# Block attention and a gated MLP on one core: a fourth group by seven half products, and GpSimd with part of the elementwise work

## The chip, the core and the metric

The kernel runs on one core of a Trainium2 chip. The core's engines each work through their own list of instructions in order: TensorE (PE) multiplies matrices and loads weights, VectorE (DVE) and ScalarE (ACT) do elementwise work on SBUF and PSUM, GpSimd (POOL) and SyncE (SP) here issue the DMA transfers. They wait for each other at semaphores. The metric is the device time of one execution in microseconds (us).

## What is computed

An attention over chunks of 64 tokens, and a two-layer MLP with the gate h * sigmoid(beta * h) on its result:

```python
def _attn_ref(q, k, v):                       # [8, 8, 576, 64]
    scores = scale * np.matmul(q_c, k_c.transpose(0, 1, 2, 4, 3))   # per chunk of 64
    scores = scores - np.max(scores, axis=-1, keepdims=True)
    attn = np.exp(scores)
    attn = attn / (np.sum(attn, axis=-1, keepdims=True) + 1e-09)
    out = np.matmul(attn, v_c)
    return out.reshape(B, H, S, D).astype(np.float32)

def _moe_ref(x, w_in, w_out, beta):           # x [4608, 512], w_in [512, 2048], w_out [2048, 512]
    h = x @ w_in
    g = h * (1.0 / (1.0 + np.exp(-beta * h)))
    return (g @ w_out).astype(np.float32)
```

The attention's output, with the heads side by side, is the x of the MLP.

## The kernel before

The 4608 tokens are worked in nine blocks of 512, numbered 0 to 8 (`NB` is 9, `QB` is 6). The attention of the later blocks is spread as small items between the matmuls of the earlier ones; it is finished when block 6 begins. Blocks 6, 7 and 8 then hold nothing but the MLP. In a block j of these, TensorE makes two things in turns: the first layer of block j (its "lane"), and the second layer of block j-1.

The second layer is done with Winograd's form of Strassen's scheme: 2 by 2 quarters, seven products (`emit_prod`, L585; p = 1, 2, 6, 5, 7, 3, 4, each for two token tiles t) in place of eight. VectorE makes the four sums of g that it needs (`emit_sum`, L436, the tiles `sm`), each once per block.

The first layer has 16 column tiles m of 128. A full product (`emit_m`, L372) makes one m with four matmuls of 512 columns; ScalarE applies Silu (L381) and VectorE scales the result by 1/beta into `gt` (`emit_mg`, L356). From block 6 on, four m at a time can instead be made as a group i by seven half products (`emit_q`, L484), again Winograd's form: four matmuls of 256 columns each. It needs sums of x (`emit_tx`, L465, four tiles `tx` per block) and sums of the weights (`emit_ws`, L456, four tiles per group, made once). A group goes in four steps s = 0 to 3 with the half products (1, 2), (6, 5), (7, 3) and (4). They are accumulated in two PSUM tiles, `qx` and `qz`; after 1, 6 and 5 ScalarE copies a state of these to the SBUF tile `hq` (L503), after 2, 7 and 3 VectorE adds one (L506), so a later half product must not write before the earlier state is taken. Then ScalarE applies Silu (`emit_q_silu`, L513: two instructions for each of three parts), and VectorE scales by 1/beta into `gt` (`emit_q_scale`, L527: two instructions for each half r of a group).

Before the change blocks 6, 7 and 8 each make groups 1, 2 and 3 by half products and m = 0 to 3 by full products. The PSUM tiles `qx` and `qz` come from the pool `ps_p0` with four buffers, those of the full products from the pool `ps_r` with two. `hq` has three buffers, `tx` two.

The order is written by hand: for each block a list of items with a place between 0 and 1 is made and sorted (L745 to L801), and each engine works through its part of the list. `LANE` (L730 to L736) gives the order of full products ("m", n) and group steps ("q", i, s), spread evenly over the block; `prod` items stand between them; silus ("qs"), scalings ("qt"), big sums ("sum"), sums of x for the next block ("tx", L777) and sums of weights ("ws", L796) get places of their own:

```python
                        c, e, f = (0.98 * sum(cost[:n + d]) / sum(cost) for d in (0, 1, 2))
...
                            items += [(e - 0.002, 2, ("qs", it[1], 2)), (f - 0.001, 2, ("qs", it[1], 1)),
                                      (f + 0.03, 3, ("qt", it[1], 0))]
...
                    if j + 1 < NB:
                        items += [(0.70 + 0.06 * n, 5, ("tx", j + 1, n)) for n in range(4)]
```

After block 8's list the rest of block 8's second layer follows (L852 to L858): the halves of the sums that are still open, then products 2, 6, 5, 7, 3 and 4, with the last stores.

GpSimd issues all loads from memory; its last one is issued long before block 6. It does no arithmetic on tiles apart from an identity matrix at the start. SyncE issues the transposes by DMA and the stores.

Of the kernel before, what the change touches and what calls it, by code (L numbers as in the profile page):

```python
# [8 lines left out]
FP32 = mybir.dt.float32  # L9
FP16 = mybir.dt.float16  # L10
ACTF = mybir.ActivationFunctionType
ALU = mybir.AluOpType
# [3 lines left out]
def kernel(  # L16
# [10 lines left out]
    nc = tc.nc  # L27
# [25 lines left out]
    ps_p0, ps_x, ps_s0 = [p.__enter__() for p in ps_open]  # L53
    ps_p, ps_s = [ps_p0], [ps_s0]
# [11 lines left out]
    ws = {i: [big.tile([128, 2, 256], FP16, name=f"ws{i}{n}") for n in range(4)] for i in (1, 2, 3)}  # L66
# [14 lines left out]
    QB = 6  # L81
# [376 lines left out]
    def emit_tx(j, n):  # L458
        if n == 0:
            tx_t[j] = [qs_p[1].tile([128, 2, 4, CH], FP16, tag=f"tx{n}", name=f"tx{n}", bufs=2) for n in range(4)]  # L460
        tx = tx_t[j]
        xq = xt_t[j].rearrange("p t (r k) (c q) -> p k c (t r) q", r=2, c=2)
        b11, b12, b21, b22 = (xq[:, :, c, 4 * r:4 * r + 4, :] for c in range(2) for r in range(2))
        in0, in1 = ((b12, b11), (b22, tx[0]), (b22, b12), (b21, tx[1]))[n]
        nc.vector.tensor_tensor(out=tx[n], in0=in0, in1=in1, op=ALU.subtract)  # L465

    qz_t = {}

# [22 lines left out]
    def emit_q(j, i, s):  # L491
        if j not in gt_t:
            gt_t[j] = gt_p.tile([128, KFF, 512], FP16, tag="gt", name="gt")
        if s == 0:
            qz_t[j, i] = [ps_p0.tile([128, 2, 256], FP32, tag="p", name=n) for n in ("qx", "qz")]
            qz_t[j, i] += [
                qs_p[0].tile([128, 4, 2, 256], FP32, name="hq")]
        x, z, hq = qz_t[j, i]
        for p in ((1, 2), (6, 5), (7, 3), (4,))[s]:
            emit_q_prod(j, i, p)  # L500
            if p in (1, 6, 5):
                o = {1: hq[:, 0:2, 0], 6: hq[:, 0:2, 1], 5: hq[:, 2:4, 1]}[p]
                nc.scalar.copy(out=o, in_=z if p == 5 else x)  # L503
            if p in (2, 7, 3):
                o = {2: hq[:, 0:2, 0], 7: hq[:, 2:4, 1], 3: hq[:, 0:2, 1]}[p]
                nc.vector.tensor_tensor(out=o, in0=x if p == 7 else z, in1=o, op=ALU.add)  # L506
# [16 lines left out]
    def emit_q_scale(j, i, r):  # L523
        hq = qz_t[j, i][2]
        for b in (2 * r, 2 * r + 1):
            m = 4 * i + b
            nc.vector.tensor_scalar(  # L527
                out=gt_t[j][:, m, :], in0=hq[:, b].rearrange("p c q -> p (c q)"),
                scalar1=rb[:, m:m + 1], scalar2=None, op0=ALU.mult)

# [83 lines left out]
    with tc.manual_schedule():  # L614
# [3 lines left out]
        for a, eng, dst in ((0, nc.sync, raw0), (1, nc.gpsimd, qk0[1])):  # L618
            for i, src in enumerate((q, k)):
                eng.dma_start(  # L620
                    out=dst[i],
# [97 lines left out]
        def att_items(u, a0, w):  # L719
            it = [(a0, 2, ("sc", u)), (a0 + 0.36 * w, 3, ("pv", u)), (a0 + 0.361 * w, 3, ("norm", u, 0)),  # L720
                  (a0 + (0.42 if u >= WV else 0.50) * w, 3, ("norm", u, 1))]
            if u >= WV:
# [7 lines left out]
        LANE = [(("m", 0), ("q", 1, 0), ("m", 1), ("q", 1, 1), ("q", 2, 0), ("q", 1, 2), ("q", 2, 1), ("q", 1, 3), ("q", 2, 2),  # L730
# [7 lines left out]
        for j in range(1, NB):  # L738
# [6 lines left out]
            items = []  # L745
# [6 lines left out]
            else:  # L752
                m0 = {2: 0.36, 4: 0.09}.get(j, 0.02)
                if j < QB:
                    items += [(m0 + (1 - m0) * m / KFF, 0, ("m", m)) for m in range(KFF)]
                else:
                    lane = LANE[2 if j == QB else j == NB - 1]
                    cost = [1 if it[0] == "q" and it[2] == 3 else 2 for it in lane]
                    for n, it in enumerate(lane):
                        c, e, f = (0.98 * sum(cost[:n + d]) / sum(cost) for d in (0, 1, 2))  # L760
                        items.append((c, 0, it))
                        if it[0] == "m":
                            items.append((c + 0.04, 3, ("mg", it[1])))
                        elif it[0] == "last":
                            pass
                        elif it[2] == 2:
                            if it[1] == 3:
                                f = e
                            items += [(e - 0.002, 2, ("qs", it[1], 2)), (f - 0.001, 2, ("qs", it[1], 1)),
                                      (f + 0.03, 3, ("qt", it[1], 0))]  # L770
                        elif it[2] == 3:
                            items += [(c + 0.001, 2, ("qs", it[1], 0)), (c + 0.04, 3, ("qt", it[1], 1))]
                    if j == QB:
                        items.append((0.01, 6, ("open",)))
                        items += [(0.011+0.001*n, 6, ("tx", QB, n)) for n in range(4)]
                    if j + 1 < NB:
                        items += [(0.70 + 0.06 * n, 5, ("tx", j + 1, n)) for n in range(4)]  # L777
                for i, p in enumerate((1, 2, 6, 5, 7, 3, 4)):
                    for t in range(2):
                        w = 1.06 if j == NB - 1 else 0.98  # L780
# [9 lines left out]
                if j == 2:  # L790
                    items += [(c, 3, ("wt", i)) for i, c in ((2, 0.36), (3, 0.55))]
                    items += [(0.07, 2, ("sc", 5)), (0.08, 2, ("xp", 4, 0)), (0.12, 2, ("xp", 4, 1)),
                              (0.17, 2, ("pv", 5)), (0.18, 3, ("norm", 5, 0)), (0.19, 3, ("norm", 5, 1)),
                              (0.27, 3, ("T", 6)), (0.53, 3, ("T", 7)), (0.60, 3, ("T", 8)), (0.61, 3, ("T", 9)), (0.80, 3, ("T", 10)),
                              (0.30, 2, ("xp", 5, 0)), (0.32, 2, ("xp", 5, 1))]
                for jw, i, c, d in ((3, 2, 0.10, 0.22), (4, 1, 0.21, 0.22), (4, 3, 0.10, 0.22)):  # L796
                    if jw == j:
                        items += [(c + d * n, 5, ("ws", i, n)) for n in range(4)]
# [92 lines left out]
```

## Time and profile before

| what | us |
|---|---|
| median of 3 runs (lowest to highest) | 275.88 (275.48 to 276.67) |
| the profiled execution's own time | 276.16 |
| its span, first to last instruction | 274.4 |
| TensorE busy | 266.0 |
| VectorE busy | 209.7 |
| ScalarE busy | 167.5 |
| GpSimd busy | 95.4 |
| first layer, L372, 488 matmuls | 106.1 |
| scalings of the groups, L527, 36 instructions | 16.2 |
| sums of x, L465, 12 instructions | 5.0 |

The times are read so: the span is what the profile covers, and the execution's time is 1.76 us longer. The granted TensorE clock was 1.00 over the whole span. A matmul's busy time overlaps with that of the next one, since they are pipelined; from start to start, four matmuls of 512 columns take 0.86 us and eight of 256 take 0.87. The busy time of a GpSimd row is rough.

### The profile page before, as it was taken

The numbers are of one execution on the slowest core, as the hardware profiler recorded it, in microseconds if no ns is written. First come the engines' busy times: TensorE is split into PE (matmuls) and PEld (weight loads), VectorE is DVE, ScalarE is ACT, GpSimd is POOL, SyncE is SP. The second block draws the span as 40 slices with busy tenths as digits, with TensorE's granted clock in tenths as the row PEclk, the third lists the DMA queues.
The fourth block names the chain that finished last, engine by engine and source line by source line (L and its number), as shares of the span: only waits on it lengthen the run. The fifth ranks groups of instructions, "written<-read, shape, count | busy, mean of one in ns | idle before, by whom it ended". The sixth has DMA issues, their size and how long they took to land.

```text
span 274.4 us, 7822 instructions
## 1 busy us (share of the span) xinstructions
PE 266.0 (97%) x3237; PEld 184.9 (67%) x3237; DVE 209.7 (76%) x394; ACT 167.5 (61%) x300; POOL 95.4 (35%) x122
## 2 busy tenths in 40 slices
PE   7789999999999999999999999999999999999995
PEld 3565445857656666666666666668887887788874
DVE  3558755899998688677977887659888778877951
ACT  3278515886555566556655656567778496759621
POOL 8954387579639955323436210000000000000000
PEclk9999999999999999999999999999999999999999
DMA  9999999999999999999999999966112102110223
GB/s 137 164 194 202 192 174 178 245 169 169 169 164 155 159 173 153 193 145 141 155 154 193 134 143 201 153 155 118 38 41 76 41 0 79 38 41 1 78 79 115
DMA packets 141763, 36.43 MB, mean 133 GB/s; under 512 B 125856, under 2 KB 141216, under 8 KB 141728
## 3 DMA queue, kind: packets, MB, share of 16 engines
q0 software_dynamic: 99136, 18.10, 83.0%
q1 hardware_dynamic: 42592, 17.84, 36.4%
q8 instruction: 25, 0.41, 0.6%
q14 instruction: 10, 0.08, 0.1%
HBM read 36.71 MB, written 9.44 MB: 168 GB/s over the span
## 4 chain that ended last, share of the span: by engine, by line
PE 67%; DMA 14%; DVE 10%; POOL 5%; issue 2%; ACT 2%; DVEq 0%; POOLq 0%
PE hps L372 23%; PE ya L585 14%; PE yb L585 14%; PE qx L484 5%; DMA wout<-in_moe_w_out_dram 5%; PE qz L484 4%; PE acc L585 4%; DMA qu<-in_q_dram 3%; DMA win<-in_moe_w_in_dram 3%; DMA ku<-in_k_dram 3%; DVE sm L436 3%; DVE gt L360 2%; POOL vbig L120 2%; PE sc L219 1%; POOL qu L112 1%
## 5 line engine op out<-in xcount | busy, mean ns | idle before, releaser
L372 PE MATMUL hps<-xt,win 128*128 128x512 f16 (+1 forms) x488 | 106.1, 355 | 0.9 <-DMA win<-in_moe_w_in_dram 0.7
L384 ACT ACTIVATE sg<-hps,bt 128x512 f32<-128x512 f32 (+1 forms) x111 | 69.5, 635 | 34.3 <-PE hps L372 31.9
L360 DVE SCALAR_TENSOR_TENSOR gt<-sg,hps 128x512 f16<-128x512 f32 (+1 forms) x111 | 67.7, 617 | 27.1 <-ACT sg L384 26.2
L372 PEld LDWEIGHTS <-win 128*128 128x128 f16 x488 | 46.2, 98 | 32.3 <-DMA win<-in_moe_w_in_dram 1.2
L585 PEld LDWEIGHTS <-sm 128*128 128x128 f16 x512 | 49.5, 98 | 12.2 <-issue 0.3
L585 PEld LDWEIGHTS <-gt 128*128 128x128 f16 x384 | 36.8, 98 | 10.6 <-DVE gt L527 0.6
L120 POOL DMA_DIRECT2D vbig<-in_v_dram x40 | 34.1, 870 | 21.8 <-DMA ku<-in_k_dram 6.3
L106 POOL DMA_DIRECT2D qu<-in_q_dram x20 | 17.1, 873 | 20.6 <-DMA qT<-qu 6.0
L513 ACT ACTIVATE hq<-hq,bs 128x256 f32<-128x256 f32 (+1 forms) x36 | 19.9, 610 | 5.5 <-DVE hq L506 5.5
L527 DVE TENSOR_SCALAR gt<-hq,rb 128x512 f16<-128x512 f32 x36 | 16.2, 481 | 6.0 <-ACT hq L513 5.3
L106 POOL DMA_DIRECT2D ku<-in_k_dram x20 | 17.1, 883 | 10.2 <-DMA qu<-in_q_dram 5.1
L436 DVE TENSOR_TENSOR sm<-gt 128x2048 f16<-128x2048 f16 (+1 forms) x17 | 19.6, 1155 | 0.3
L585 PE MATMUL yb<-wt,sm 128*128 128x256 f16 x152 | 19.7, 273 | 0.1
L585 PE MATMUL ya<-wt,sm 128*128 128x256 f16 x152 | 19.7, 273 | 0.0
L484 PEld LDWEIGHTS <-ws 128*128 128x128 f16 x144 | 14.1, 98 | 1.6
L241 ACT ACTIVATE et<-sc 128x1024 f16<-128x1024 f32 (+1 forms) x10 | 8.3, 852 | 10.5 <-PE sc L232 10.4
L397 PE MATMUL ops<-wout,gt 128*128 128x512 f16 x64 | 14.7, 380 | 0.0
L585 PE MATMUL yb<-wout,gt 128*128 128x256 f16 x104 | 13.9, 273 | 0.2
L585 PE MATMUL ya<-wout,gt 128*128 128x256 f16 x104 | 13.6, 273 | 0.0
L506 DVE TENSOR_TENSOR hq<-qz,hq 128x512 f32<-128x512 f32 x18 | 12.3, 683 | 1.1 <-ACT hq L503 0.8
L503 ACT COPY hq<-qx 128x512 f32<-128x512 f32 x18 | 10.5, 581 | 2.9 <-PE qx L484 2.7
L278 DVE TENSOR_TENSOR x<-x,rx 128x512 f16<-128x512 f32 (+1 forms) x20 | 11.9, 620 | 0.3
(100 smaller groups left out, 354.3 us busy)
## 6 DMA issues: line engine op xcount, KB each, us to landing
out_dram<-osb SPq DMA_DIRECT2D x32, 256.0 KB, 2.9
vbig<-in_v_dram POOLq DMA_DIRECT2D x32, 128.0 KB, 7.6
qu<-in_q_dram POOLq DMA_DIRECT2D x18, 128.0 KB, 11.5
ku<-in_k_dram POOLq DMA_DIRECT2D x18, 128.0 KB, 8.3
win<-in_moe_w_in_dram POOLq DMA_DIRECT2D x8, 256.0 KB, 9.5
wout<-in_moe_w_out_dram POOLq DMA_DIRECT2D x4, 512.0 KB, 12.2
qu<-in_q_dram POOLq DMA_DIRECT2D x5, 256.0 KB, 6.5
ku<-in_k_dram POOLq DMA_DIRECT2D x5, 256.0 KB, 6.8
```

Of the source, the lines that this page charges most:

```text
L106: nc.gpsimd.dma_start(out=tv[off:off + n, sp], in_=src[b, :, s:s + n, :].rearrange("h p d -> p h d"),)
L120: nc.gpsimd.dma_start(out=vbig[off:off + n, i % NV, :, 0:D], in_=v[b, :, s:s + n, :].rearrange("h p d -> p h d"),)
L360: nc.vector.scalar_tensor_tensor(out=gt_t[j][:, m, c0:c0 + n], in0=sg[:, 0:n], scalar=1.0, in1=hps[:, 0:n], op0=ALU.add, op1=ALU.mult,)
L372: nc.tensor.matmul(out=hps[:, 0:n], lhsT=w_in16[m // 2][:, kk, (m % 2) * 128:(m % 2) * 128 + 128], rhs=xr[:, c0 // CH:(c0 + n) // CH, 2 * ...
L384: nc.scalar.activation(out=sg[:, 0:n], in_=hps[:, 0:n], func=ACTF.Tanh, scale=bt[:, m:m + 1])
L397: nc.tensor.matmul(out=ops, lhsT=gt_t[j][:, kk, t * 128:(t + 1) * 128], rhs=w_out16[kk // 4][:, kk % 4, :], start=(kk == 0), stop=(kk == K ...
L436: nc.vector.tensor_tensor(out=sm[i][:, lo:hi, :], in0=a, in1=b, op=op)
L484: nc.tensor.matmul(out=dst[:, s, :], lhsT=lhsT, rhs=rhs, start=(p in (1, 2, 5) and s == 0 and kk == 0), stop=(s == 1 and kk == 1), skip_gr ...
L506: nc.vector.tensor_tensor(out=o, in0=x if p == 7 else z, in1=o, op=ALU.add)
L513: nc.scalar.activation(out=o, in_=src, func=ACTF.Silu, scale=bs[:, m:m + 1])
L527: nc.vector.tensor_scalar(out=gt_t[j][:, m, :], in0=hq[:, b].rearrange("p c q -> p (c q)"), scalar1=rb[:, m:m + 1], scalar2=None, op0=ALU. ...
L585: nc.tensor.matmul(out=dst, lhsT=lhsT, rhs=rhs, start=(p in (1, 2, 5) and kk == 0 and (t == 0 or last)), stop=(kk == 7 and (t == 1 or last ...
```

## The change

Six things change.

1. In block 7 all 16 column tiles are made by half products: group 0 joins groups 1, 2 and 3, and the four full products are gone. The lane of block 7 (`LANE[0]`) is written anew, and spread over 0.96 of the block instead of 0.98.
2. In block 7 the two PSUM tiles of group 2 come from `ps_r`, which the full products no longer use there.
3. The four sums of weights of group 0 are made by VectorE in block 6.
4. GpSimd instead of VectorE makes the sums of x for blocks 7 and 8; their places in the list are earlier (0.40 to 0.70 in place of 0.70 to 0.88).
5. In each group of blocks 6, 7 and 8, GpSimd makes the first of the four scalings (b = 0).
6. In all three blocks the Silu items of part 2 are placed a little earlier (0.02 ahead of e instead of 0.002), and the scalings of r = 0 a little later (0.04 after f instead of 0.03).

```diff
-        nc.vector.tensor_tensor(out=tx[n], in0=in0, in1=in1, op=ALU.subtract)
+        (nc.gpsimd if j > QB else nc.vector).tensor_tensor(out=tx[n], in0=in0, in1=in1, op=ALU.subtract)
...
-            qz_t[j, i] = [ps_p0.tile([128, 2, 256], FP32, tag="p", name=n) for n in ("qx", "qz")]
+            qz_t[j, i] = [(ps_p[0] if j == 7 and i == 2 else ps_p0).tile([128, 2, 256], FP32, tag="p", name=n) for n in ("qx", "qz")]
...
-            nc.vector.tensor_scalar(
+            (nc.gpsimd if r == 0 and b % 2 == 0 else nc.vector).tensor_scalar(
                 out=gt_t[j][:, m, :], in0=hq[:, b].rearrange("p c q -> p (c q)"),
                 scalar1=rb[:, m:m + 1], scalar2=None, op0=ALU.mult)
...
-        LANE = [(("m", 0), ("q", 1, 0), ("m", 1), ("q", 1, 1), ("q", 2, 0), ("q", 1, 2), ("q", 2, 1), ("q", 1, 3), ("q", 2, 2),
-                 ("q", 3, 0), ("q", 2, 3), ("q", 3, 1), ("m", 2), ("q", 3, 2), ("m", 3), ("q", 3, 3)),
+        LANE = [(("q", 1, 0), ("q", 0, 0), ("q", 2, 0), ("q", 1, 1), ("q", 1, 2), ("q", 0, 1), ("q", 0, 2), ("q", 2, 1), ("q",
+                 1, 3), ("q", 0, 3), ("q", 2, 2), ("q", 3, 0), ("q", 2, 3), ("q", 3, 1), ("q", 3, 2), ("q", 3, 3)),
...
+                    ls = 0.96 if j == 7 else 0.98
                     for n, it in enumerate(lane):
-                        c, e, f = (0.98 * sum(cost[:n + d]) / sum(cost) for d in (0, 1, 2))
+                        c, e, f = (ls * sum(cost[:n + d]) / sum(cost) for d in (0, 1, 2))
...
-                            items += [(e - 0.002, 2, ("qs", it[1], 2)), (f - 0.001, 2, ("qs", it[1], 1)),
-                                      (f + 0.03, 3, ("qt", it[1], 0))]
+                            items += [(e - 0.02, 2, ("qs", it[1], 2)), (f - 0.001, 2, ("qs", it[1], 1)),
+                                      (f + 0.04, 3, ("qt", it[1], 0))]
...
-                        items += [(0.70 + 0.06 * n, 5, ("tx", j + 1, n)) for n in range(4)]
+                        items += [(0.40 + 0.10 * n, 5, ("tx", j + 1, n)) for n in range(4)]
...
+                if j == 6:
+                    items += [(0.30 + 0.10 * n, 5, ("ws", 0, n)) for n in range(4)]
```

## The prediction

> **What bounds the kernel now.** The first view is the page's head: the sums by engine, and the span in 40 slices of 6.86 us.
>
> ```profile
> PE 266.0 (97%) x3237; PEld 184.9 (67%) x3237; DVE 209.7 (76%) x394; ACT 167.5 (61%) x300; POOL 95.4 (35%) x122
> ...
> PE   7789999999999999999999999999999999999995
> ...
> POOL 8954387579639955323436210000000000000000
> ```
>
> TensorE is full from the fourth slice on; GpSimd is empty from the 25th, after its last load. The change touches only blocks 6, 7 and 8 (nine blocks, counted from 0). I found their borders in the timeline and asked for busy time in each; the fourth row is the products left after block 8's lane.
>
> ```profile
> core 0: us, PE busy (x) PEld busy (x) DVE busy (x) ACT busy (x) POOL busy (x), PEclk, DMA share, GB/s
> 183.30:208.20 24.90, 24.90 (x228) 20.76 (x216) 22.13 (x42) 17.98 (x35) 0.00 (x0) 1.00 0.32 81
> 208.20:233.20 25.00, 25.00 (x215) 20.68 (x214) 20.51 (x37) 17.78 (x36) 0.00 (x0) 1.00 0.13 43
> 233.20:258.20 25.00, 25.00 (x215) 20.70 (x213) 20.51 (x35) 17.50 (x36) 0.00 (x0) 1.00 0.10 33
> 258.20:271.40 13.20, 12.85 (x113) 10.63 (x111) 7.71 (x15) 4.71 (x13) 0.00 (x0) 1.00 0.30 101
> ```
>
> A block of 25.0 us holds 25.0 us of TensorE at clock 1.00, so a matmul taken away is time taken away. But VectorE is busy for 82 to 89% of a block, and TensorE has little patience with it. The view of waits, for weight loads in this stretch, shows where VectorE already makes TensorE stop:
>
> ```profile
> PEld L585 <- DVE gt L527: 0.6, 2, 0.3
> PEld L585 <- DVE gt L356: 0.4, 2, 0.2
> ```
>
> Two waits on L356 are at the borders 6 to 7 and 7 to 8 (a product of 1.14 us at 209.08, of 1.14 at 234.03, where others have 1.04); two on L527 are in the tail at 260.75 and 261.15. Hidden waits have short slack. An example from block 7: the second half product of a group (qz) may not be overwritten until VectorE has added it, and VectorE has scalings ahead of that addition.
>
> ```profile
> 224.02 0.60 PE L484 MATMUL qz<-xt,win 128*128 128x256 f16 x4
> ...
> 226.20 0.60 PE L484 MATMUL qz<-tx,ws 128*128 128x256 f16 x4
> ```
> ```profile
> 224.20 0.87 DVE L527 TENSOR_SCALAR gt<-hq,rb 128x512 f16<-128x512 f32 x2
> 225.13 0.69 DVE L506 TENSOR_TENSOR hq<-qz,hq 128x512 f32<-128x512 f32 x1
> ```
>
> The addition ends at 225.82, TensorE overwrites at 226.20: slack 0.38 us. At the same place in block 6 (addition 200.17 to 200.86, qz at 201.25) it is 0.39.
>
> **The change, part by part.**
>
> *TensorE.* In block 7 four full products (L372: 16 matmuls of 512 columns) become a fourth group (L484: 28 of 256). In the chain of waits four of the first kind take 0.86 us and eight of the second 0.87: 4 x 0.865 = 3.46 against 28 x 0.109 = 3.05, so **-0.41 us**. Twelve more weight loads at 0.098 us lie under matmuls of 0.109; uncovered they would cost up to 1.2.
>
> *ScalarE.* Four Silu of 685 ns go; three copies (581), two Silu each of 474, 502 and 717 ns come: 5.1 - 2.7 = +2.4 us in block 7, where it works 17.8 of 25.0 us. The cover is its idle 7.2 us; without it the copies that free qx and qz would be late, and TensorE with them. I price it at 0.
>
> *VectorE.* Away go eight sums of x (about 0.34 us from start to start) and ten of 47 scalings (0.40): 2.7 + 4.0. Added are four sums of weights in block 6 (0.34) and three additions (0.60): 1.4 + 1.8. It is relieved by 3.5 us in 75; where it is not what TensorE waits for this is worth nothing. The weight sums are put among the last two big sums of block 6, of which the third has 4.0 us of slack (done 193.74, first used 197.76); that covers 1.4.
>
> *Order.* At block 6's tight place three scalings now stand ahead of the addition instead of two: +0.40 against the slack of 0.39, so 0 to 0.1 us.
>
> *Buffers and queues.* Group 2 of block 7 takes its two PSUM buffers from the pool that the full products leave. The fourth group's first ScalarE copy waits for GpSimd's scaling of the first group, and other ScalarE work queues behind it; some eight lane items (about 10 us) lie between. No DMA is added, and SyncE's list stays. GpSimd's 18 instructions stand behind all its loads, so no load is delayed; among themselves sums of x queue behind scalings that wait for ScalarE, but each is needed several us later.
>
> *GpSimd's own durations* are shown by no row of these forms. The nearest ones:
>
> ```profile
> masks.py:199 POOL TENSOR_SCALAR_AFFINE_SELECT ident<-ident 128x128 f16<-128x128 f16 x1 | 0.3, 290 | 0.1
> L875 POOL MEMSET const-bfloat16-1.0<- 128x1 bf16 x1 | 0.1, 102 | 0.0
> L527 DVE TENSOR_SCALAR gt<-hq,rb 128x512 f16<-128x512 f32 x36 | 16.2, 481 | 6.0 <-ACT hq L513 5.3
> ```
>
> A fixed 0.10 and 0.19 for 128 columns give 0.86 us for 512, all of it scaled by four gives 1.16: estimates, of which I take 1.0 for a scaling. Below, VectorE's 0.48 is the end; above, twice 1.16 = 2.3 if 4-byte input or a second input doubles it. A sum of x has two inputs: 0.86 to 2.3, I take 1.2.
>
> *What the engines do to each other.* The trace has no GpSimd arithmetic beside VectorE. The low end is no effect: a big sum at 66.36 took 1.23 us beside GpSimd's DMA issues, 1.22 without. The high end is that one stands while the other works. The scalings meet by construction: of a pair released by the same two Silu, GpSimd gets the first and VectorE the second. VectorE's pair took 0.80; 1.0 of standing plus 0.40 is **+0.6**. The issue row speaks for 0, but issuing is no reading of tiles, so I take half, 0.3. Then the border 6 to 7 and the tail, without slack, lose 0.3 each, block 6's tight place 0.3 (its slack being spent on the third scaling), block 7's nothing (0.3 under 0.38): +0.9. A fourth meeting is early in block 6: the first two sums of x of block 7 need only their data, whose last transposes are issued at 178.10 to 183.25 and land some 3.7 us later, so about when VectorE makes its own sums of x (185.88) and the big sums from 188.55. The second big sum ends at 191.01 and is used at 191.21. Half of 1.2 less 0.2 would be 0.4; since the two may also run before, I take 0.2. The border 7 to 8 loses its wait for a full product's scaling, at most 0.1 gained, left out.
>
> The Trainium skill ("SBUF — State Buffer", Who interferes with whom) says that a VectorE instruction with two SBUF inputs, or in a two-port mode as a scaling can be, and a GpSimd instruction that reads SBUF exclude each other for the whole instruction. By that the term is the full one and the sum that of the first rival; no run here shows it yet. Its "GPSIMD Engine Reference" (Elementwise — side-by-side cycle accounting) puts one-input work at 1.03 to 1.8 cycles an element at 1.2 GHz, an estimate of 0.44 to 0.77 us for 512; with that a pair would lose at most 0.4, and the sum would be nearer to no change.
>
> **Sum:** -0.41 + 0.9 + 0.2 = +0.7 us. The profiled execution took 276.16 (span 274.40, 1.76 around it), 0.28 over the median of 275.88. Its span would be 275.1; on the median the forecast is **276.6 us**, no change by what a measurement of this kernel can tell (0.5%, 1.4 us).
>
> **Rivals.**
> *Full exclusion* (the other side, slower). Place: VectorE's queue ahead of the tight places; price 0.6 per pair; it decides once what it adds passes 1.8 us, that is 0.41 and 1.4. Border and tail 0.6 each; block 6's place 0.6 + 0.01; block 7's 0.6 - 0.38 = 0.22; the early meeting 1.2 - 0.2 = 1.0: 3.03 - 0.41 = +2.6, **278.5**. For it: pairs start together, and VectorE has 82% to do. Against it: the 1.23 us sum.
> *No effect.* TensorE's 0.41 is kept less 0.1 at block 6: -0.3, **275.6**. For it: VectorE is relieved by 3.5 us. Against: the tail keeps its waits, since ScalarE paces the last scalings. Faster by 1.4 would need the 0.41 and all 1.0 of the shown waits gone.
> *GpSimd twice as slow.* Scalings of 2.3 with full exclusion cost 1.3 more at four places: 2.6 + 5.2 = +7.8, **283.7**; if only two of the places are met, 281.1. For it: 4-byte input; against: nothing but the small row.
>
> **How the numbers follow.** Forecast 0.36 (0.05 of it above 277.3), full exclusion 0.33 (0.01 of it under 277.3), no effect 0.22 (0.03 of it faster by over 0.5%, for the shown runs span 1.2 us), twice as slow 0.09. Slower: 0.05 + 0.32 + 0.09 = 0.46. Same: 0.31 + 0.01 + 0.19 = 0.51. Faster 0.03. The range reaches from no effect less some measuring spread, 275.3, to full exclusion with one more meeting of 1.3, 279.8; outside lie about 0.05 below and 0.13 above. The forecast's own range is 275.8 (one meeting of 0.3 alone) to 277.5 (0.9 more in all).
>
> **What would show it.** Block 7 must hold 24.6 us of TensorE work; if it lasts 24.6, the first step is right. GpSimd's rows give L465 and L527 their durations: 1.2 and 1.0. L527 and the big sums on VectorE tell the exclusion: at 0.48 and 1.22 there is none, and rows stretched towards 1.0 or gaps ahead of them, with no releaser, are the full one. New waits of weight loads or matmuls on VectorE should stand at block 6's second big sum and last group, the border 6 to 7 and the tail. Wrong would be waits on ScalarE in block 7, or TensorE waiting for GpSimd itself.

## The result and the profile after

The changed kernel takes 277.05 us (median of 9 runs, 276.96 to 277.86) against 275.60 for the kernel before on the same chip (9 runs, 275.02 to 276.67): a ratio of 1.0051, 95% interval 1.0039 to 1.0064, so 1.4 us slower. The profiled execution took just the median time (277.05), with a span of 275.3.

First the sums by engine and one of the rows of 40 slices, from the page of the changed kernel:

```profile
PE 265.8 (97%) x3249; PEld 185.9 (68%) x3249; DVE 210.4 (76%) x383; ACT 168.8 (61%) x305; POOL 121.1 (44%) x140
...
POOL 8964478489639945333436200030344093204200
```

GpSimd now has work after the 25th slice. VectorE, which was to be relieved, is busy for 210.4 us where it was busy for 209.7, with eleven instructions fewer. Next the busy time of each engine in blocks 6, 7, 8 and the rest (the borders are put at the same matmuls as for the kernel before):

```profile
core 0: us, PE busy (x) PEld busy (x) DVE busy (x) ACT busy (x) POOL busy (x), PEclk, DMA share, GB/s
182.95:208.30 25.35, 25.15 (x233) 20.80 (x219) 22.77 (x39) 18.09 (x36) 8.33 (x7) 1.00 0.31 85
208.30:234.02 25.72, 24.98 (x227) 21.88 (x225) 21.90 (x32) 18.91 (x41) 11.30 (x8) 1.00 0.13 42
234.02:259.33 25.31, 25.16 (x216) 20.88 (x214) 20.17 (x32) 18.60 (x38) 4.69 (x3) 1.00 0.10 33
259.33:272.44 13.11, 12.67 (x112) 10.39 (x109) 7.00 (x13) 4.36 (x12) 1.57 (x1) 1.00 0.30 101
```

Block 7 was to shrink from 25.0 to 24.6 us; it lasts 25.72. Block 6 has grown by 0.45 us and block 8 by 0.31. The clock is 1.00 as before. The waits from 183 us on, first those of weight loads, then those of matmuls (us in total, times, longest):

```profile
PEld L484 <- issue: 1.5, 3, 0.8
PEld L585 <- DVE gt L527: 0.5, 2, 0.3
PEld L585 <- DVE gt L356: 0.4, 1, 0.4
...
```
```profile
PE qz L484 <- DVE hq L506: 0.8, 2, 0.6
PE yb L585 <- DVE gt L356: 0.2, 1, 0.2
```

New are the waits of the half products (L484): the matmul waits for VectorE's addition (L506) to take the state of `qz`, and the weight load behind it stands for "issue" only because the matmul does. TensorE never waits for GpSimd or ScalarE.

For an account that adds up I took the starts of all matmuls from block 6's first half product to the last matmul, and subtracted from each distance what the matmul needs, 0.2165 us for 512 columns and 0.1092 for 256. What remains are the times in which TensorE stood; these are worked out from the trace, not lines of it:

| place | before | after | forecast for the difference |
|---|---|---|---|
| block 6, last group, `qz` | 0 | 0.37 | +0.3 |
| border 6 to 7 | 0.09 | 0.32 | +0.3 |
| block 7, last group, `qx` and `qz` | 0 | 0.88 | 0 |
| border 7 to 8 | 0.09 | 0 | 0 |
| block 8, group 1, `qz` | 0 | 0.31 | 0 |
| tail | 0.78 | 0.69 | +0.3 |
| early in block 6 | 0 | 0 | +0.2 |
| all gaps | 0.98 | 2.59 | +1.1 |
| first to last matmul | 85.96 | 87.16 | +0.7 |

The matmuls alone took 0.41 us less, as forecast; the gaps grew by 1.61: together the +1.20 of the last row. (The two medians differ by 1.45, the two profiled spans by 0.9, since the stretch ahead of block 6 varies by some tenths between executions: its first half product starts at 185.10 us before and at 184.78 after.) The rows by form of VectorE and of GpSimd say who did it (busy us, mean ns of one):

```profile
L436 DVE TENSOR_TENSOR sm<-gt 128x2048 f16<-128x2048 f16 x15 | 18.3, 1217 | 0.2
L527 DVE TENSOR_SCALAR gt<-hq,rb 128x512 f16<-128x512 f32 x30 | 17.9, 641 | 8.6 <-ACT hq L513 8.2
...
L356 DVE TENSOR_SCALAR gt<-sg,rb 128x512 f16<-128x512 f32 x7 | 3.8, 548 | 0.2
```
```profile
L527 POOL TENSOR_SCALAR gt<-hq,rb 128x512 f16<-128x512 f32 x10 | 15.6, 1564 | 51.9 <-ACT hq L513 51.9
...
L465 POOL TENSOR_TENSOR tx<-xt,tx 128x512 f16<-128x512 f16 x4 | 5.3, 1324 | 0.1
L465 POOL TENSOR_TENSOR tx<-xt 128x512 f16<-128x512 f16 x4 | 5.1, 1285 | 26.0 <-DMA xt<-x 26.0
```

VectorE's scalings, 481 ns each before, now take 641 and 548: 30 x 0.16 + 7 x 0.067 = 5.3 us. That is more than the 3.5 us of work it gave away. Where it went is seen best at block 7's tight place, in the timelines of VectorE, GpSimd and TensorE there (start us, us, engine, line):

```profile
224.60 2.58 DVE L527 TENSOR_SCALAR gt<-hq,rb 128x512 f16<-128x512 f32 x3 [1.87 <-ACT hq L513]
...
229.70 0.68 DVE L506 TENSOR_TENSOR hq<-qz,hq 128x512 f32<-128x512 f32 x1
```
```profile
224.06 1.56 POOL L527 TENSOR_SCALAR gt<-hq,rb 128x512 f16<-128x512 f32 x1 [0.31 <-ACT hq L513]
225.59 1.31 POOL L465 TENSOR_TENSOR tx<-xt 128x512 f16<-128x512 f16 x1
```
```profile
229.25 0.60 PE L484 MATMUL qx<-tx,ws 128*128 128x256 f16 x4
230.43 0.60 PE L484 MATMUL qz<-tx,ws 128*128 128x256 f16 x4 [0.58 <-DVE hq L506]
```

Three scalings that need 1.28 us (two take 0.87 to 0.88, so 0.40 from start to start, and 0.48 for the last) took 2.58. The second ended 0.28 us after GpSimd's scaling, the third 0.28 after GpSimd's sum of x. VectorE has no pause from there to the addition at 229.70, so what the two meetings cost, 1.30 us, reaches the addition. How much of it TensorE feels is told by the run with nothing on GpSimd (the first experiment), which has the same lane. There the addition ends at 228.27 and TensorE overwrites `qz` at 228.40, so the slack of this lane is 0.13 us, not the 0.38 of the old one. Counted against TensorE's work, the addition comes 0.96 us later in the changed kernel than in that run, so 0.83 should come through. TensorE's gaps there are 0.04, 0.10 and 0.74.

### The profile page after: what moved, and what is told of

It is laid out like the page before. It is cut to its first block, busy times and chain, and to the rows that moved or that the text cites. A ratio compares the mean times of both kernels' runs of the same rounds, so it can differ in the third digit from the quotient of the medians.

```text
span 275.3 us, 7880 instructions
## 1 busy us (share of the span) xinstructions
PE 265.8 (97%) x3249; PEld 185.9 (68%) x3249; DVE 210.4 (76%) x383; ACT 168.8 (61%) x305; POOL 121.1 (44%) x140
## 4 chain that ended last, share of the span: by engine, by line
PE 71%; DVE 15%; DMA 6%; ACT 3%; issue 3%; POOL 2%; DVEq 0%; ACTq 0%; POOLq 0%
PE hps L372 26%; PE yb L585 13%; PE ya L585 11%; PE ops L397 5%; PE qx L484 4%; PE acc L585 4%; PE qz L484 3%; DMA qu<-in_q_dram 3%; DVE sm L436 3%; DVE gt L527 3%; DMA ku<-in_k_dram 3%; DVE gt L360 2%; ACT hq L513 2%; DVE hq L506 2%; PE sc L219 1%
## 5 line engine op out<-in xcount | busy, mean ns | idle before, releaser
L372 PE MATMUL hps<-xt,win 128*128 128x512 f16 (+1 forms) x472 | 102.2, 354 | 0.4 <-ACT xt L333 0.2
L372 PEld LDWEIGHTS <-win 128*128 128x128 f16 x472 | 44.8, 98 | 30.5 <-issue 0.4
L120 POOL DMA_DIRECT2D vbig<-in_v_dram x40 | 34.1, 871 | 24.6 <-DMA ku<-in_k_dram 7.7
L527 POOL TENSOR_SCALAR gt<-hq,rb 128x512 f16<-128x512 f32 x10 | 15.6, 1564 | 51.9 <-ACT hq L513 51.9
L513 ACT ACTIVATE hq<-hq,bs 128x256 f32<-128x256 f32 (+1 forms) x40 | 22.1, 611 | 8.0 <-DVE hq L506 8.0
L527 DVE TENSOR_SCALAR gt<-hq,rb 128x512 f16<-128x512 f32 x30 | 17.9, 641 | 8.6 <-ACT hq L513 8.2
L484 PEld LDWEIGHTS <-ws 128*128 128x128 f16 x160 | 15.6, 98 | 3.4 <-issue 1.5
L465 POOL TENSOR_TENSOR tx<-xt 128x512 f16<-128x512 f16 x4 | 5.1, 1285 | 26.0 <-DMA xt<-x 26.0
L506 DVE TENSOR_TENSOR hq<-qz,hq 128x512 f32<-128x512 f32 x20 | 13.6, 681 | 0.5 <-ACT hq L503 0.4
L503 ACT COPY hq<-qx 128x512 f32<-128x512 f32 x20 | 11.6, 582 | 3.1 <-PE qx L484 2.9
```

The lines of the kernel that those rows point to most:

```text
L120: nc.gpsimd.dma_start(out=vbig[off:off + n, i % NV, :, 0:D], in_=v[b, :, s:s + n, :].rearrange("h p d -> p h d"),)
L372: nc.tensor.matmul(out=hps[:, 0:n], lhsT=w_in16[m // 2][:, kk, (m % 2) * 128:(m % 2) * 128 + 128], rhs=xr[:, c0 // CH:(c0 + n) // CH, 2 * ...
L484: nc.tensor.matmul(out=dst[:, s, :], lhsT=lhsT, rhs=rhs, start=(p in (1, 2, 5) and s == 0 and kk == 0), stop=(s == 1 and kk == 1), skip_gr ...
L513: nc.scalar.activation(out=o, in_=src, func=ACTF.Silu, scale=bs[:, m:m + 1])
L527: (nc.gpsimd if r == 0 and b % 2 == 0 else nc.vector).tensor_scalar(out=gt_t[j][:, m, :], in0=hq[:, b].rearrange("p c q -> p (c q)"), scal ...
```

## The experiments

The theory under test, called the port theory in the expectations: a GpSimd instruction holds VectorE's instructions that work from SBUF to SBUF while it runs, and that alone makes the loss; the fourth group is worth its 0.41 us. Rivals: the fourth group itself costs (its order, ScalarE's 2.4 us, the Silus moved), or it is the number of instructions on VectorE's queue.

**Nothing on GpSimd.** Both lines of GpSimd's part are undone; the fourth group, the order and the places in the list stay.

```diff
-        (nc.gpsimd if j > QB else nc.vector).tensor_tensor(out=tx[n], in0=in0, in1=in1, op=ALU.subtract)
+        nc.vector.tensor_tensor(out=tx[n], in0=in0, in1=in1, op=ALU.subtract)
...
-            (nc.gpsimd if r == 0 and b % 2 == 0 else nc.vector).tensor_scalar(
+            nc.vector.tensor_scalar(
```

> The changed kernel without GpSimd's part: sums of x and scalings all on VectorE, the fourth group and the new order kept. Theory 'port': no scaling is stretched (L527 at 481 ns throughout), the waits at qz in blocks 6, 7 and 8 (0.37, 0.75, 0.30 us) shrink to what VectorE's own load makes of them; with 3.2 us more work on it than in the kernel before, 0 to 0.9 us slower than before, ratio 1.000 to 1.0035. Theory 'order': the waits stay where they are and the ratio is that of the changed kernel, 1.005, or above it.

Measured: 275.01 us (11 runs) against 275.45, ratio 0.9989 (0.9977 to 1.0001). Busy time in block 7, and VectorE's scalings:

```profile
core 0: us, PE busy (x) PEld busy (x) DVE busy (x) ACT busy (x) POOL busy (x), PEclk, DMA share, GB/s
...
207.40:232.00 24.60, 24.60 (x227) 21.85 (x225) 21.87 (x39) 18.65 (x40) 0.00 (x0) 1.00 0.13 44
```
```profile
L527 DVE TENSOR_SCALAR gt<-hq,rb 128x512 f16<-128x512 f32 x40 | 17.5, 482 | 5.8 <-ACT hq L513 5.2
```

Block 7 lasts 24.60 us and is full; from the first half product to the last matmul it is 85.55 us, 0.41 less than before, with the same gaps (0.97). So the fourth group costs nothing beside its saving, though VectorE is busier here than before (21.87 us against 20.51), and the whole loss is GpSimd's part. The port theory's own number was too careful: it had put 0 to 0.9 us of loss on VectorE's larger load, and there was none. Since the interval reached 1.000, the same kernel ran again in more rounds:

> The changed kernel with nothing on GpSimd, again and in more rounds. Theory (the 0.41 us of block 7 is kept whole): ratio 0.9985, with an interval that ends below 1. Rival (the first 0.9989 was spread between runs): an interval around 1.000.

274.98 (12 runs) against 275.40, ratio 0.9990 (0.9979 to 1.0000), with gaps of 0.97 again. The interval touches 1, so neither statement of the expectation is shut out by the times; the two traces show the 0.41 us. This is the fastest version found.

**One half of GpSimd's part at a time.** With the scalings alone on GpSimd (only the first hunk above):

> The changed kernel with all sums of x back on VectorE; GpSimd keeps the ten scalings. Theory 'port': each GpSimd scaling of 1.56 us still holds VectorE's second and third scaling of the group; L527 on VectorE stays between 520 and 600 ns, ratio to before 1.003 to 1.006. Theory 'order': VectorE has 2.7 us more to do than in the changed kernel, ratio 1.005 to 1.010, with L527 at 481 ns.

276.31 (10 runs), ratio 1.0025 (1.0013 to 1.0037). The time lies a little under the theory's 1.003 to 1.006. The gaps are 1.76 us: the border 6 to 7 0.31, block 7 0.32, block 8 0.42, the tail 0.70. The rows:

```profile
L527 DVE TENSOR_SCALAR gt<-hq,rb 128x512 f16<-128x512 f32 x30 | 14.5, 527 | 8.2 <-ACT hq L513 7.9
...
L527 POOL TENSOR_SCALAR gt<-hq,rb 128x512 f16<-128x512 f32 x10 | 16.5, 1654 | 86.3 <-ACT hq L513 86.3
```

VectorE's 527 ns lie in the expected 520 to 600. GpSimd's scalings are held too: two of the ten take 1.89 and 2.14 us, the other eight 1.56. In this run and the next 2.2 us of each execution lie outside its span, where all others have 1.7 to 2.0; some 0.45 us of their times therefore belongs to no gap. By the spans alone (medians of all executions) this kernel takes 274.05 us against 273.7 for the kernel before.

The scalings are worth 1.76 - 0.97 = 0.79 us of gaps, the sums of x, added to them, another 2.59 - 1.76 = 0.83. So one would think that the sums alone cost 0.8 (only the second hunk above):

> The changed kernel with all scalings back on VectorE; GpSimd keeps the sums of x of blocks 7 and 8. Theory 'port' (a VectorE scaling that starts while GpSimd works on tiles stands until GpSimd's instruction ends): only the eight sums are left to hold it; the second wait of 0.75 us at qz in block 7 becomes small, since no GpSimd scaling stands there, L527 on VectorE falls from a mean of 641 to under 550 ns; 0.3 to 1.0 us faster than the changed kernel, ratio to before 1.001 to 1.004. Theory 'order' (the new lane, the third scaling ahead of the addition and ScalarE's load make the waits, not GpSimd): VectorE gets 4.0 us of work back, so the waits stay or grow, ratio 1.005 to 1.010.

278.24 (277.07 to 279.57, 6 runs), ratio 1.0103 (1.0077 to 1.0129): above every number I had put down, and by the median worse than both halves together, also when only the spans are compared (276.0 against 275.3). The executions differ by 2.5 us, and the shortest is no longer than the changed kernel's median. The profiled one took 279.31, and its gaps, 4.57 us, are those of a long execution. The timelines of GpSimd and VectorE at the beginning of block 6 show why, and the wait is that of `qz`:

```profile
183.35 1.15 POOL L465 TENSOR_TENSOR tx<-xt 128x512 f16<-128x512 f16 x1 [26.27 <-DMA xt<-x]
184.58 1.15 POOL L465 TENSOR_TENSOR tx<-xt,tx 128x512 f16<-128x512 f16 x1
185.70 1.33 POOL L465 TENSOR_TENSOR tx<-xt 128x512 f16<-128x512 f16 x1
186.99 1.33 POOL L465 TENSOR_TENSOR tx<-xt,tx 128x512 f16<-128x512 f16 x1
```
```profile
185.41 0.60 DVE L465 TENSOR_TENSOR tx<-xt 128x512 f16<-128x512 f16 x1
186.05 1.26 DVE L465 TENSOR_TENSOR tx<-xt,tx 128x512 f16<-128x512 f16 x1
187.23 1.37 DVE L465 TENSOR_TENSOR tx<-xt 128x512 f16<-128x512 f16 x1
188.53 0.41 DVE L465 TENSOR_TENSOR tx<-xt,tx 128x512 f16<-128x512 f16 x1
```
```profile
PE qz L484 <- DVE hq L506: 1.5, 1, 1.5
```

In the changed kernel GpSimd's scalings stand in its queue between the sums of x and hold the later ones back until ScalarE has released a group. Without them all four run as soon as their data are there, in a row, beside VectorE's own sums of x for block 6: three of those take 0.60, 1.26 and 1.37 us in place of 0.42, and the first additions of block 6 are late by it (1.64 us of gap). Block 8's four (three at 203.3 to 207.5, the last at 210.2) hold scalings ahead of the border in the same way (1.63). The scheduling by GpSimd's queue was not in my theory.

Two tests of this reading. The same kernel, with a scaling of one column by GpSimd into a scratch tile in front of VectorE's two scalings of r = 0, so that the sums are kept apart:

```diff
+        if r == 0:
+            scr = qs_p[1].tile([128, 8], FP16, tag="scr", name="scr", bufs=2)
+            nc.gpsimd.tensor_scalar(
+                out=scr[:, 0:1], in0=hq[:, 0, 0, 0:1],
+                scalar1=rb[:, 4 * i:4 * i + 1], scalar2=None, op0=ALU.mult)
```

> The changed kernel with all scalings on VectorE, as in the first experiment, but with a scaling of one column (scratch, about 0.1 us) left in GpSimd's list where the scalings stood, so that the sums of x are kept apart as in the changed kernel. Theory 'bunching' (the first experiment lost 3.6 us of TensorE because four sums in a row held VectorE at 183 to 188 and again at 203 to 207): sums apart hold it one at a time, TensorE's waits fall from 4.57 to 1.3 to 2.5 us, ratio 1.001 to 1.005. Rival 'VectorE's own load' (it lost because ten scalings came back to VectorE): the waits stay at 4 to 5 us, ratio 1.009 to 1.012.

277.29 (7 runs, 277.01 to 280.17), ratio 1.0092 (1.0056 to 1.0127); two executions of some 280 us raise this ratio, the medians alone give 1.0065. The profiled execution is one of the two (279.80), but what it has too much stands ahead of block 6, whose first half product starts at 187.08 where it was at 183.8 to 185.1 in the other runs. From there on no gap is left early in block 6, and its sums of x by VectorE are back at 417 to 422 ns; the border 6 to 7 (0.84) and block 7 (0.58, 0.11 and 0.74) have gaps instead. The gaps fall from 4.57 to 3.05, not to the expected 1.3 to 2.5: the row of four explains the beginning of block 6, and sums kept apart still meet scalings. The ratio lies in the range of the rival, VectorE's own load; but that load is the same with nothing on GpSimd, where the gaps are 0.97. And the opposite, all eight sums placed early in block 6, with a third buffer, so that blocks 7 and 8 are free of them:

```diff
-            tx_t[j] = [qs_p[1].tile([128, 2, 4, CH], FP16, tag=f"tx{n}", name=f"tx{n}", bufs=2) for n in range(4)]
+            tx_t[j] = [qs_p[1].tile([128, 2, 4, CH], FP16, tag=f"tx{n}", name=f"tx{n}", bufs=3) for n in range(4)]
...
-                    if j + 1 < NB:
-                        items += [(0.40 + 0.10 * n, 5, ("tx", j + 1, n)) for n in range(4)]
+                    if j == QB:
+                        items += [(0.02 + 0.30 * (jj - 7) + 0.001 * n, 5, ("tx", jj, n)) for jj in (7, 8) for n in range(4)]
```

> The fourth group kept, all scalings on VectorE, and GpSimd makes the sums of x of blocks 7 and 8 early in block 6, where VectorE has no group's scalings (three buffers for tx in place of two). Theory 'port': nothing is left for GpSimd to hold but VectorE's two-input sums; L527 at 481 ns, waits of TensorE as in the kernel before (about 1.0 us), and its 0.41 us of matmuls is kept: 0.1 to 0.5 us faster than before, ratio 0.998 to 1.000. Theory 'order': the lane costs what it cost, ratio 1.003 to 1.005.

279.28 (4 runs), ratio 1.0135 (1.0114 to 1.0156), the slowest of all, where I had expected no loss. The gaps are 5.32 us: 1.67 early in block 6, as with four sums in a row above, then 1.05 at the second big sum and 1.06 at the next group. The second set of sums runs as soon as its data land. VectorE, then GpSimd, at the second big sum:

```profile
191.28 2.06 DVE L436 TENSOR_TENSOR sm<-sm,gt 128x2048 f16<-128x2048 f16 x1
193.27 1.37 DVE L356 TENSOR_SCALAR gt<-sg,rb 128x512 f16<-128x512 f32 x1
```
```profile
190.95 1.31 POOL L465 TENSOR_TENSOR tx<-xt 128x512 f16<-128x512 f16 x1 [2.65 <-DMA xt<-x]
192.34 2.02 POOL L465 TENSOR_TENSOR tx<-xt,tx 128x512 f16<-128x512 f16 x1
```

A big sum of 1.22 us takes 2.06 behind one sum of x, GpSimd's next sum of x is held in turn until the big sum has ended at 193.34 and takes 2.02, and the scaling after it is held by that one.

**GpSimd's part without the fourth group.** The kernel before with the two GpSimd lines alone; its sums of x keep their later places.

> The kernel before with GpSimd's part of the change alone (sums of x for blocks 7 and 8, and the scalings of b = 0 in the first half of each group); block 7 keeps its four full products, the places in the list stay. Theory (GpSimd holds VectorE's scalings whatever the lane of block 7 looks like): the gaps between TensorE's matmuls from block 6 on grow from 0.98 us by 1.2 to 2.0, none of it paid back by the 0.41 us of the fourth group, so a ratio to the kernel before of 1.004 to 1.008. Rival (the holding costs only because the fourth group makes block 7 tighter: 0.84 us of the 1.61 stand at one place in block 7): the gaps grow by 0.5 to 0.9, ratio 1.001 to 1.003.

277.59 (4 runs) against 275.40, ratio 1.0076 (1.0062 to 1.0091). The gaps are 3.00 us, 2.02 more than before, nearly all of it in two waits of matmuls at the two borders:

```profile
PE ya L585 <- DVE gt L356: 1.0, 1, 1.0
PE yb L585 <- DVE gt L356: 1.0, 1, 1.0
```

The ratio lies inside the theory's 1.004 to 1.008 and the gaps just past its 1.2 to 2.0; the rival's numbers do not hold: the loss needs no fourth group. VectorE and GpSimd ahead of the first border:

```profile
204.87 1.29 DVE L356 TENSOR_SCALAR gt<-sg,rb 128x512 f16<-128x512 f32 x1
...
208.96 0.48 DVE L527 TENSOR_SCALAR gt<-hq,rb 128x512 f16<-128x512 f32 x1 [1.60 <-ACT hq L513]
209.53 0.72 DVE L356 TENSOR_SCALAR gt<-sg,rb 128x512 f16<-128x512 f32 x1
```
```profile
204.72 1.15 POOL L465 TENSOR_TENSOR tx<-xt 128x512 f16<-128x512 f16 x1
...
208.41 1.56 POOL L527 TENSOR_SCALAR gt<-hq,rb 128x512 f16<-128x512 f32 x1 [1.24 <-ACT hq L513]
```

One meeting of a sum of x with a scaling (1.29 in place of 0.48) makes the additions after it late, these make ScalarE's Silus late, and the scaling that the border waits for stands behind the Silus and is itself held (0.72) by GpSimd's scaling. It also tells that the fourth group and the other places of the sums, together, make the changed kernel less bad than GpSimd's part by itself (gaps of 2.59 against 3.00); which of the two does it was not tried.

**Is it holding, or what was taken from VectorE?** To the kernel before nine scalings by GpSimd are added that nobody reads; VectorE keeps all its work.

```diff
+        if r == 0:
+            scr = qs_p[1].tile([128, 512], FP16, tag="scr", name="scr", bufs=2)
+            nc.gpsimd.tensor_scalar(
+                out=scr, in0=hq[:, 0].rearrange("p c q -> p (c q)"),
+                scalar1=rb[:, 4 * i:4 * i + 1], scalar2=None, op0=ALU.mult)
```

> The kernel before, untouched in its work, with nine more GpSimd instructions: a second copy of each group's first scaling, into a scratch tile that nobody reads. VectorE is relieved of nothing. Theory 'port': a GpSimd scaling of about 1.56 us holds VectorE's scalings that start in its later part; L527 on VectorE (36 of 481 ns) rises to 510 to 580 ns, and TensorE's waits grow by 0.2 to 1.0 us: ratio 1.001 to 1.004. Rival 'moved work' (the loss in the changed kernel comes from GpSimd's results being late or from the order of VectorE's list, not from the engines holding each other): L527 stays at 481 ns, ratio 1.000 within its interval.

276.68 (9 runs) against 275.49, ratio 1.0046 (1.0029 to 1.0062); VectorE's 36 scalings take 556 ns each instead of 481, and the gaps grow by 0.78 us, as much as by the scalings in the test above (0.79). The ratio is a little above the theory's 1.004, and of the 1.19 us between the times the gaps account for these 0.78 only. So it is GpSimd's working beside VectorE that costs, not what was taken from VectorE. The same with nine fills of 1023 columns, each behind a scaling of one column, in place of the nine scalings, to see whether GpSimd has to read for it:

```diff
+            scr = qs_p[1].tile([128, 1024], FP16, tag="scr", name="scr", bufs=2)
...
+            nc.gpsimd.memset(scr[:, 1:1024], 0.0)
```

> The kernel before with GpSimd work that reads next to nothing: at each of the nine places a scaling of one column and then a fill of 1023 columns of a scratch tile with zeros. Theory 'port' in its form 'reading': a fill does not hold VectorE, L527 stays at 481 ns, ratio 1.000 (0.999 to 1.001). In its form 'any GpSimd instruction that touches SBUF': VectorE's scalings stretch as beside a scaling, L527 over 510 ns, ratio 1.001 to 1.004.

278.68 (4 runs), ratio 1.0117 (1.0094 to 1.0140): a fill that reads nothing does more harm than a scaling, more than either form had put down, and the gaps are 3.95 us. Reading is not needed. The scaling of one column in front of each fill is not what holds: in the run above that keeps the sums apart, VectorE's next scaling takes 0.49 us behind such a one where no sum of x follows (at 238.83, 252.05 and 263.23). GpSimd's and VectorE's rows by form, and one of the nine places in the timelines of both:

```profile
L530 POOL MEMSET scr<- 128x1023 f16 x9 | 8.5, 948 | 0.0
```
```profile
L533 DVE TENSOR_SCALAR gt<-hq,rb 128x512 f16<-128x512 f32 x36 | 21.8, 639 | 5.1 <-ACT hq L513 4.5
```
```profile
207.66 1.81 DVE L533 TENSOR_SCALAR gt<-hq,rb 128x512 f16<-128x512 f32 x2 [0.32 <-ACT hq L513]
```
```profile
208.24 0.95 POOL L530 MEMSET scr<- 128x1023 f16 x1
```

The fill ends at 209.18 and the second of the two scalings, 0.28 us behind it, at 209.46; it began at 208.27 and so took 1.19.

**ScalarE in GpSimd's place.** ScalarE makes the quarter of the scalings, VectorE the sums of x.

```diff
-            (nc.gpsimd if r == 0 and b % 2 == 0 else nc.vector).tensor_scalar(
+            if r == 0 and b % 2 == 0:
+                nc.scalar.activation(out=gt_t[j][:, m, :], in_=hq[:, b].rearrange("p c q -> p (c q)"),
+                                     func=ACTF.Copy, scale=rb[:, m:m + 1])
+                continue
+            nc.vector.tensor_scalar(
```

> The changed kernel with the sums of x on VectorE and the quarter of the scalings on ScalarE instead of GpSimd. Theory 'port': ScalarE holds nobody, L527 on VectorE stays at 481 ns, and VectorE is as relieved as with GpSimd; if ScalarE's ten further instructions (about 0.65 us each, 6.5 us in 75, where it works some 18.5 of 25) lie in its idle time, ratio 0.997 to 1.000. Rival 'ScalarE is late': its copies that free qx and qz are delayed by up to one scaling at each group, TensorE waits on ScalarE, ratio 1.002 to 1.008.

276.78 (7 runs) against 275.49, ratio 1.0039 (1.0024 to 1.0055). VectorE's 30 scalings are at 482 ns, so ScalarE doesn't hold them; but the gaps are 2.53 us, in block 6 (0.44), at the beginning of block 7 (0.30), at its tight place (0.51) and in the tail (one gap of 0.52 where it was 0.23). TensorE mostly waits for VectorE's additions and scalings again, but now VectorE waits: it is idle for 10.4 us ahead of its scalings, nearly all of it for ScalarE's Silus, where it was 5.8 with nothing on GpSimd. At the beginning of block 7 TensorE waits for ScalarE itself: the half product at 210.40 stands until a Silu that ends at 210.35 has read its PSUM tile. ScalarE works in order and pays for the scalings by being late with the rest. The rival's ratio holds; its wait, of TensorE on ScalarE, is the smaller part, and most of the lateness reaches TensorE through VectorE.

**A fourth group in block 8 too.** From the version with nothing on GpSimd: block 8's lane is block 7's with the last products of block 7 kept in their places, and group 2's PSUM tiles come from the other pool in block 8 as well.

```diff
-            qz_t[j, i] = [(ps_p[0] if j == 7 and i == 2 else ps_p0).tile([128, 2, 256], FP32, tag="p", name=n) for n in ("qx", "qz")]
+            qz_t[j, i] = [(ps_p[0] if j >= 7 and i == 2 else ps_p0).tile([128, 2, 256], FP32, tag="p", name=n) for n in ("qx", "qz")]
...
-                (("m", 0), ("q", 1, 0), ("m", 1), ("q", 1, 1), ("q", 2, 0), ("m", 2), ("q", 1, 2), ("q", 2, 1), ("m", 3), ("q",
-                 1, 3), ("q", 2, 2), ("q", 3, 0), ("q", 2, 3), ("q", 3, 1), ("last", 1, 0), ("q", 3, 2), ("last", 1, 1), ("q", 3,
-                 3)),
+                (("q", 1, 0), ("q", 0, 0), ("q", 2, 0), ("q", 1, 1), ("q", 1, 2), ("q", 0, 1), ("q", 0, 2), ("q", 2, 1), ("q", 1, 3), ("q", 0, 3), ("q", 2, 2), ("q", 3, 0), ("q", 2, 3), ("q", 3, 1), ("last", 1, 0), ("q", 3, 2), ("last", 1, 1), ("q", 3, 3)),
```

> The changed kernel with nothing on GpSimd, and block 8 too makes group 0 by half products (its four full products go). Theory (TensorE's saving is per block, and VectorE and ScalarE have room when GpSimd is left out): another 0.41 us of matmuls, gaps as before at about 1.0, ratio 0.997. Rival (block 8 ends in the tail, where ScalarE and VectorE set the end, and its lane holds the last products of block 7 too): gaps of 1.4 us or more, ratio 0.9985 or above.

276.02 (11 runs), ratio 1.0022 (1.0012 to 1.0032): slower than with one block. The matmuls give another 0.41 us, the gaps grow to 2.05:

```profile
PE qz L484 <- ACT hq L513: 0.6, 1, 0.6
PE qx L484 <- ACT hq L503: 0.2, 1, 0.2
```

The rival's numbers hold, but not its place: the tail has the same 0.78 us as before. At the beginning of block 8 the half product at 234.90 stands for 0.72 us until block 7's last Silu, which ends at 234.85, has read its PSUM tile. At 242.73 another stands for 0.40 us until ScalarE has copied `qx`, a copy that comes behind two Silus. ScalarE is busy for 19.2 of the 24.7 us of this block, so the cover that the prediction named for it, idle time, is not enough by itself: it has to lie at the right place.

## Why the prediction was right or wrong, step by step

The time came out 0.45 us above the forecast, inside its own range, on the side and for the cause that the prediction gave; the size of single terms was off in both directions. The difference itself was forecast at +0.7 us and called no change; it was 1.45 by the medians and 1.20 by the trace from block 6 on, and the interval of the ratio lies wholly above 1.

- *TensorE, -0.41:* right to the hundredth. Block 7 holds 24.60 us of work when nothing holds VectorE.
- *ScalarE's 2.4 us priced at 0:* right; no wait on ScalarE in block 7. The 2.4 themselves were too much: ScalarE's busy time in block 7 rose by 1.1 us (17.78 to 18.91), since the durations that were summed overlap.
- *VectorE's relief of 3.5 us, worth nothing:* right as a price, and wrong as a relief, since 5.3 us of standing took its place.
- *GpSimd's durations:* 1.2 for a sum of x was right (1.15 alone, 1.29 to 1.32 on average). 1.0 for a scaling was too little: 1.56 in every case of the changed kernel, inside the bounds of 0.48 and 2.3.
- *Order at block 6's tight place, together with half a pair there, 0.3 to 0.4:* measured 0.37, by other parts and so by luck. Three scalings took 2.17 us in place of 1.28, the second held by a sum of x. VectorE had reached them 0.45 us earlier, so against block 6's first half product the addition is 0.71 us later; less the slack of 0.39, that is 0.32.
- *Border 6 to 7, 0.3:* measured 0.23. The scaling of L356 took 0.72 us in place of 0.48, held by the end of GpSimd's scaling.
- *Tail, 0.3:* measured -0.09. Beside GpSimd's last scaling (from 259.65) VectorE's next one is free, the one after is held by only 0.20, and VectorE has one of 0.40 less to make.
- *Early meeting, 0.2:* nothing. GpSimd's two sums were done at 185.77, before VectorE's own began to matter (one took 0.48 in place of 0.42). The clause "the two may also run before" was the right one; the experiments with four in a row show what the other case costs, 1.6 us.
- *Block 7's tight place, "nothing (0.3 under 0.38)":* **the step that failed.** The price per meeting was a half-length average over pairs of scalings. What happens is no average: the end of GpSimd's scaling cost 0.41 and the sum of x right behind it 0.89, 1.30 in all. The slack of 0.38 was read off the lane that the change writes anew; the new lane's is 0.13, so that even the half meeting of 0.3 would have come through. Meetings of sums of x with scalings, away from the early one, were in no term of the sum, though the change puts them at 0.40 to 0.70 of blocks 6 and 7, where VectorE scales.
- *Block 8:* not in the forecast either; 0.31, of which 0.10 stands there with nothing on GpSimd too, and 0.21 comes from a held scaling (three took 1.68).

The sum came near by luck: the two terms that were too high (tail, early meeting: 0.6 together) stood against the two that were missing (blocks 7 and 8: 1.2). Of the rivals, *full exclusion* named what happens when a sum of x meets a scaling, but its places were wrong (nothing early in block 6, nothing in the tail); *no effect* falls by the stretched rows, *twice as slow* by 1.56. The rule cited from the Trainium skill ("SBUF — State Buffer", Who interferes with whom), that the later of the two waits for the whole instruction of the earlier one, agrees with this case for a GpSimd sum against a VectorE scaling (1.38 in place of 0.48) and against a big sum (2.06), and for the fill; it doesn't for GpSimd's scaling, below. The figures of the Trainium skill ("GPSIMD Engine Reference", Elementwise — side-by-side cycle accounting) that gave an estimate of 0.44 to 0.77 us for one-input work do not fit the 1.56 us measured.

## What to carry to other kernels

Before work is moved from VectorE to GpSimd, list which VectorE instructions will run at the same time: those that work from SBUF to SBUF can stand until GpSimd's instruction ends (here a scaling of 0.48 us took up to 1.48), so a relief of 3.5 us was met by 5.3 of standing. Price a meeting at the full remaining length, place by place, against the slack of the next addition or scaling that TensorE waits for, as the new order leaves it, and take GpSimd's queue order as part of the price: what stands between two of its instructions decides whether they come one by one or in a row. Test the parts of a combined change alone: the fourth group by itself kept its 0.41 us.

## What the runs showed of the hardware that I had not expected

- A held VectorE scaling ends 0.28 us after the end of the GpSimd instruction, whichever that is: ten cases in the changed kernel behind sums of x and scalings, 0.27 to 0.29 each, and all nine cases behind the fills. VectorE's additions with one input in PSUM are never longer than 0.69 us beside GpSimd.
- GpSimd's scaling does not hold over its whole length. In the changed kernel VectorE scalings that start 0.55 us after it take 0.49, as always; those that start 0.94 to 1.2 us after it stand until its end. Where GpSimd's scaling is itself held and takes 1.8 to 2.1 us (the scalings alone on GpSimd, and the copies that nobody reads), its end is what counts: a VectorE scaling that starts 0.3 to 0.6 us before it stands until it, one that starts 0.94 us before it takes 0.48. The first part is not free either: a sum of weights that starts 0.41 us after GpSimd's scaling takes 0.56 us in place of 0.42 (changed kernel, at 201.16), and beside the copies VectorE scalings that start 0.48 to 0.54 us after it take 0.70 to 0.74. A big sum in the same stretch is free, here in the timeline of VectorE and then of GpSimd:

```profile
221.12 0.49 DVE L527 TENSOR_SCALAR gt<-hq,rb 128x512 f16<-128x512 f32 x1
221.52 1.22 DVE L436 TENSOR_TENSOR sm<-gt,sm 128x2048 f16<-128x2048 f16 x1
```
```profile
220.57 1.56 POOL L527 TENSOR_SCALAR gt<-hq,rb 128x512 f16<-128x512 f32 x1 [9.85 <-ACT hq L513]
222.10 1.65 POOL L465 TENSOR_TENSOR tx<-xt,tx 128x512 f16<-128x512 f16 x1
```

  The sum of x that follows on GpSimd is held by that same big sum until 222.74 (1.65 in place of 1.15), so holding goes both ways. There are five such cases in the changed kernel, beside that big sum and beside scalings: each time the sum of x ends 1.00 to 1.01 us after VectorE's instruction. That the last 0.6 us of a scaling is its writing, which would fit the fill and the free big sum, is an explanation that no run here isolates.
